# Attention on one core: one head per PSUM bank, the denominators' addition on ScalarE, and the weight conversion elsewhere in the order

## The chip, the cores and the metric

The kernel runs on one core of one Trainium2 chip. The metric is the device time of one execution in microseconds (us), median of several runs. The profile is of one execution; its times count from the first instruction. PE is TensorE's matmuls, PEld its weight loads, DVE VectorE, ACT ScalarE, POOL GpSimd, and SP SyncE, which issues most transfers.

## The reference

The program is linear attention with a feature map, followed by two feed-forward layers. Only the first part is touched by the change:

```python
def phi(x):                       # x: (4 batches, 8 heads, 576 tokens, 64 channels)
    proj = np.einsum('bhsd,df->bhsf', x, w_phi)          # 64 channels -> 128 features
    proj = proj - np.max(np.abs(proj), axis=-1, keepdims=True)
    return np.concatenate([np.exp(proj), np.exp(-proj)], axis=-1)
q_p, k_p = phi(q), phi(k)
kv  = np.einsum('bhsf,bhsd->bhfd', k_p, v)
z   = np.sum(k_p, axis=2)
num = np.einsum('bhsf,bhfd->bhsd', q_p, kv)
den = np.einsum('bhsf,bhf->bhs', q_p, z)[..., None] + 1e-06
attn = num / den
...
x = attn as (2304 tokens, 512)
g = h * clip(h + 3, 0, 6) / 6 with h = x @ w_in;  x = g @ w_out        # 512 -> 2048 -> 512
# then a mixture of 8 experts with a gate, on the same 2304 tokens
```

## The kernel before, in words

Attention works on 16 units `u`, each a pair of heads of one batch (576 tokens each). A unit's k and q come in one load as 9 blocks of 128 columns: blocks 0 to 3 are k, block 4 holds the last 64 tokens of both heads of k and of q, blocks 5 to 8 are q. The rows (partitions) of the blocks are 64 channels twice. Before the change, row half `e` of block `a` holds token block `2a + e` of the flat list of both heads' eight blocks, so each half holds blocks of both heads.

`proj` (lines 230 to 258) multiplies both row halves with `w_phi`, four 64x64 matmuls at a time, into two PSUM banks `pj`, one per row half; then, bank after bank, VectorE takes the maximum of the absolute values (line 257) and subtracts it (line 258) into `dd`, where `e` is the third index. It runs for three groups of blocks: P0 (k, four blocks), P1 (block 4), P2 (q, four blocks). `kexp` (E0, E1: one head each; E2: the rest) takes exponentials of `dd` and of its negative into `kp` on ScalarE (lines 265, 266). `kv_mm` (KV, line 280) multiplies `kp` with `v`, the two heads into two column halves, head 0 first in each round. `z_sum` (S0, S1, line 290) adds on GpSimd, and `z_mm` (Z, line 300) sums over tokens on TensorE, behind KV in the same bank `pkv`. `kv_cp` (C, line 312) copies that bank to SBUF on ScalarE, `kv_tr` (KT) transposes it, sums the z halves on VectorE (line 323) and copies the rest on ScalarE to `kvz` (line 331). `q_tr` (Q0, Q1, Q2) transposes q's part of `dd` and takes its exponentials (lines 344, 349) to `qp`. `num` (N0, N1, line 395) and `den` (D, line 359) are the two products; the addition of 1e-6 is on VectorE (line 369), and a transfer turns the result to `rt`. One period later `den2` (R) takes the reciprocal (line 376), writes it to DRAM, reads it back spread over rows as `rr` (line 381), and, in its second step, GpSimd multiplies the numerators with it (line 385).

Meanwhile the weights of the first feed-forward layer are converted from float64 bits in 16 pieces, one a period, by `split_w` (lines 132 to 169). It is a generator whose first step is the load. Its next four, each called "w" in the order, are: absolute value on ScalarE (line 154) with a maximum on GpSimd (line 155); a shift on VectorE (line 157); a second VectorE operation (line 159); a third (line 161) with two on GpSimd (lines 168, 169). The intermediates `f` and `m` have one buffer each, the raw words two.

The order on TensorE, VectorE, ScalarE and GpSimd is written out by hand as a list of names and kept; the transfers of SP are ordered by the program's scheduler. A period of iteration `it` finishes unit `it` and prepares unit `it + 1`:

```python
seq = ("KV Z C Q0 Q0 Q1 Q1 Q2 Q2 KT KT KT R P0 P0 E0 S0 E1 S1 P1 P1 E2 P2 P2 w "
       "N0 N0 N1 N1 D D w R w w").split()
```

A name that stands twice or three times is a generator: its first place issues the first part (matmuls, transposes, transfers), its later ones the evacuations. In iteration 14 the D are left out; in iteration 15 (`seq15`) they come as `d`. PSUM has eight buffers under the tag "b", given out in turn. After iteration 15 the feed-forward layer begins; its instructions are not in the hand-written order.

Of the kernel before, what the change touches and what calls it, by code (L numbers as in the profile page):

```python
# [17 lines left out]
P = 128  # L18
# [171 lines left out]
def step(g):  # L190
    return next(g, None)
# [7 lines left out]
def attention(tc, a, ident, xT, wA, rt_last, late):  # L199
    nc = tc.nc  # L200
    with ExitStack() as ctx:
# [4 lines left out]
        pl = E(name="apl", bufs=2, side="left")  # L206
        p3 = E(name="ap3", bufs=1, side="left")
        ps = E(name="aps", bufs=1, space=PS)
        wbd = cst.tile([P, 256], F32, name="wbd")
        ones = cst.tile([P, 3, 32], F32, name="ones")  # L210
        nc.gpsimd.memset(ones, 1.0)
        nc.gpsimd.memset(ones[64:128, 1, :], 0.0)
# [3 lines left out]
        def load(u):  # L216
            x = p2.tile([P, 9, P], F32, tag="qk", bufs=2, name=f"qk{u}")
            if u == 0:
                nc.sync.dma_start(wbd, a["w_phi"])
                for g in range(3):  # L220
                    nc.sync.dma_start(x[:, 3 * g : 3 * g + 3], a["qk"][u][:, 384 * g : 384 * g + 384])
            else:
                nc.sync.dma_start(x.rearrange("p n t -> p (n t)"), a["qk"][u])
            t = p2.tile([P, 10, 64], F32, tag="lv", bufs=4, name=f"v{u}")
            nc.sync.dma_start(t.rearrange("p n d -> p (n d)"), a["v"][u])
            return [x, t]
# [3 lines left out]
        def proj(u, g):  # L230
            x = lds[u][0]
            if g == 0:
                st[u] = (
                    p2.tile([P, 9, 2, P], F32, tag="dd", name=f"dd{u}"),
                    p2.tile([P, 5, 2, 2, P], F32, tag="kp", name=f"kp{u}"),
                    p2.tile([P, 18], F32, tag="mx", name=f"mx{u}"),
                )
            dd, kp, mx = st[u]
            b0, n = ((0, 4), (4, 1), (5, 4))[g]
            pj = [ps.tile([P, 512], F32, tag="b", bufs=8, name=f"pj{u}_{g}_{e}") for e in range(2)]  # L240
            for j in range(n):
                for c in range(2):
                    for e in range(2):
                        rs, cs = slice(64 * e, 64 * e + 64), slice(64 * c, 64 * c + 64)
                        nc.tensor.matmul(  # L245
                            pj[e][cs, P * j : P * j + P],
                            x[rs, b0 + j, cs],
                            wbd[rs, P * e : P * e + P],
                            start=True,
                            stop=True,  # L250
                            tile_position=(64 * e, 64 * c),
                        )
            yield
            for e in range(2):
                pv = pj[e][:, 0 : P * n].rearrange("p (x f) -> p x f", f=P)
                m = mx[:, 9 * e + b0 : 9 * e + b0 + n]
                nc.vector.tensor_reduce(m, pv, axis=AX.X, op=ALU.max, apply_absolute_value=True)  # L257
                nc.vector.tensor_sub(dd[:, b0 : b0 + n, e], pv, m.unsqueeze(2).broadcast_to([P, n, P]))  # L258

        def kexp(u, g):  # L260
            dd, kp, mx = st[u]
            if g < 2:
                dv = dd[:, 2 * g : 2 * g + 2].rearrange("p a h f -> p (a h) f")
                kv_ = kp[:, 2 * g : 2 * g + 2].rearrange("p r h s f -> p (r h) s f")
                nc.scalar.activation(kv_[:, :, 0, :], dv, AF.Exp)
                nc.scalar.activation(kv_[:, :, 1, :], dv, AF.Exp, scale=-1.0)  # L266
            elif g == 2:
                nc.scalar.activation(kp[:, 4, 0, 0, :], dd[:, 4, 1, :], AF.Exp)
                nc.scalar.activation(kp[:, 4, 0, 1, :], dd[:, 4, 1, :], AF.Exp, scale=-1.0)
# [63 lines left out]
        def q_tr(u, h):  # L333
            dd = st[u][0]
            if h == 0:
                bk.setdefault(u, {})["qp"] = p3.tile([P, 2, 2, S], F32, tag="qp", name=f"qp{u}")
            qp = bk[u]["qp"]
            pq = ps.tile([P, 512], F32, tag="b", bufs=8, name=f"pq{u}_{h}")
            if h < 2:
                for r in range(4):  # L340
                    nc.tensor.transpose(pq[:, P * r : P * r + P], dd[:, 5 + 2 * h + r // 2, r % 2, :], ident)
                yield
                for s in range(2):
                    nc.scalar.activation(qp[:, s, h, 0:512], pq, AF.Exp, scale=1.0 - 2 * s)
            else:
                nc.tensor.transpose(pq[:, 0:128], dd[:, 4, 0, :], ident)
                yield
                for s in range(2):
                    nc.scalar.activation(
                        qp[:, s, :, 512:576], pq[:, 0:128].rearrange("p (h t) -> p h t", h=2), AF.Exp, scale=1.0 - 2 * s  # L350
                    )

        def den(u):
            zs, qp = bk[u]["zs"], bk[u]["qp"]
            pd = ps.tile([P, 512], F32, tag="b", bufs=8, name=f"pd{u}")
            for s in range(2):
                for g in range(4):
                    h, c = divmod(g, 2)
                    nc.tensor.matmul(
                        pd[32 * g : 32 * g + 32, 0:288],  # L360
                        zs[:, s, h, :],
                        qp[:, s, h, 288 * c : 288 * c + 288],
                        start=(s == 0),
                        stop=(s == 1),
                        tile_position=(0, 32 * g),
                    )
            yield
            dn = pl.tile([P, 288], F32, tag="dn", name=f"dn{u}")
            nc.vector.tensor_scalar_add(dn, pd[:, 0:288], 1e-6)
            rt = pl.tile([P, 9], F32, tag="rt", name=f"rt{u}") if u < NU - 1 else rt_last  # L370
            (nc.sync if u < NU - 1 else nc.gpsimd).dma_start(rt, dn[0:128:32, :].rearrange("g (j k) -> g j k", k=9))
            rts[u] = rt
# [14 lines left out]
        def num(u, c):  # L387
# [16 lines left out]

        lds, cv = {}, {}
        seq = (
            "KV Z C Q0 Q0 Q1 Q1 Q2 Q2 KT KT KT R P0 P0 E0 S0 E1 S1 P1 P1 E2 P2 P2 w "
            "N0 N0 N1 N1 D D w R w w"
        ).split()
        pre1 = "P0 P0 E0 S0 E1 S1 P1 P1 E2 P2 P2".split()  # L410
        seq14 = [op for op in seq if op != "D"]
        seq15 = "w KV Z C Q0 Q0 d Q1 Q1 d Q2 Q2 KT KT KT R w N0 N0 N1 N1 D D w R w".split()
        with tc.manual_schedule(
            engines={nc.tensor.engine, nc.vector.engine, nc.scalar.engine, nc.gpsimd.engine}
        ):
            for it in range(-1, NU):
# [9 lines left out]
                    cv[it + 1] = split_piece(tc, p3, a, wA, 0, it + 1, ("wf", "wm", 1))  # L426
                    step(cv[it + 1])
                gens = {}
                for op in {-1: pre1, NU - 2: seq14, NU - 1: seq15}.get(it, seq):
                    kd, i = op[0], int(op[1]) if op[-1].isdigit() else 0  # L430
                    if op in gens:
                        step(gens[op])
                    elif kd == "P" and nx:
                        gens[op] = proj(it + 1, i)
                        step(gens[op])
                    elif kd == "E" and nx:
                        kexp(it + 1, i)
                    elif kd == "R" and it >= 1:
                        gens[op] = den2(it - 1)
                        step(gens[op])  # L440
                    elif kd == "S" and nx:
                        z_sum(it + 1, i)
                    elif kd == "Z" and has:
                        z_mm(it)
                    elif kd == "C" and has:
                        kv_cp(it)
                    elif op == "w" and has:
                        step(cv[it])
                    elif op == "KV" and has:
                        kv_mm(it)  # L450
                    elif kd == "d":
                        gens[op] = den(it - 1)
                        step(gens[op])
                    elif has and kd in "KQND":
                        gens[op] = {"K": kv_tr, "D": den}[kd](it) if kd in "KD" else {"Q": q_tr, "N": num}[kd](it, i)
                        step(gens[op])
# [727 lines left out]
def lay_out(arrays):  # L1184
# [4 lines left out]
    q, k, v = pair(q), pair(k), pair(v)  # L1189
    qk = np.empty((NU, 2, D, 9, P), np.float32)  # L1190
    for n, x in ((0, k), (5, q)):
        x = x[:, :, 0:512].reshape(NU, 4, 2, P, D)
        qk[:, :, :, n : n + 4] = x.transpose(0, 2, 4, 1, 3)
    for i, x in enumerate((q, k)):
        qk[:, i, :, 4] = x[:, :, 512:].transpose(0, 3, 1, 2).reshape(NU, D, P)
    vv = np.zeros((NU, P, 10, D), np.float32)
    vv[:, :, 0:8] = v[:, :, 0:512].reshape(NU, 2, 4, P, D).transpose(0, 3, 1, 2, 4).reshape(NU, P, 8, D)
    wb = np.zeros((P, 2, P), np.float32)
    for h in range(2):
        vv[:, 64 * h : 64 * h + 64, 8 + h] = v[:, h, 512:]  # L1200
        wb[64 * h : 64 * h + 64, h] = w
    return {"in_qk": qk.reshape(NU, P, 9 * P), "in_v": vv.reshape(NU, P, 10 * D), "in_w_phi": wb.reshape(P, 2 * P)}


_INS = [
# [23 lines left out]
```

## Time and profile before

| what | value |
|---|---|
| median of 3 runs | 927.88 us (927.8 to 929.29) |
| the profiled execution: its own time, its span | 926.54 us, 924.5 us |
| PE, DVE, ACT, POOL busy | 882.1, 589.2, 496.4, 349.0 us |
| mean granted TensorE clock | 0.992 of full speed |
| attention | to about 196 us |

A busy share is an average over stages with different limits; the ends of matmuls are modelled, so short waits of TensorE show better in the starts of its instructions and in PEld's idle time than in PE's busy time.

### The profile page before, as it was taken

The page shows a single profiled execution, that of the slowest core. Times are in us where ns is not written, and L with a number is a line of the kernel's source. Part 1 is how long each engine was busy: PE and PEld are TensorE (multiplying, and loading weights), DVE is VectorE, ACT ScalarE, POOL GpSimd, SP SyncE. Part 2 cuts the span into 40 slices and gives each one's busy share as a digit, 9 for nine tenths or more (in the row PEclk, how much of TensorE's full clock was granted, in tenths as well). Part 3 has the DMA queues.
Part 4 walks back from the last instruction along what each step waited for, and adds up shares of the span by engine and source line. Part 5 has one row for each costly group of instructions (what it writes and reads, how often), then busy time and mean ns, then how long its engine had stood idle before and what let it go on. Part 6 is the DMA issues. An engine that isn't in the chain of part 4 may idle for free. (4 is left out here: it accounts for less than half of the span.)

```text
span 924.5 us, 16115 instructions
## 1 busy us (share of the span) xinstructions
PE 882.1 (95%) x5890; PEld 712.8 (77%) x5890; DVE 589.2 (64%) x998; ACT 496.4 (54%) x869; POOL 349.0 (38%) x244
## 2 busy tenths in 40 slices
PE   7999999979989999999999999999699999999996
PEld 4666666557878998898898988987578888888884
DVE  5888888879993433433433333456598888888882
ACT  4666666644443233233233233244488888888882
POOL 2566666654660100100000000113457766666631
PEclk9999999999999999999999999999799999999999
DMA  7454554333410200100100100541324651545530
GB/s 238 117 167 146 153 162 133 100 105 121 121 47 1 67 3 0 35 1 1 35 1 1 35 1 1 98 141 19 61 93 162 244 197 37 215 144 194 192 133 15
DMA packets 39247, 86.37 MB, mean 93 GB/s; under 512 B 10868, under 2 KB 11896, under 8 KB 39164
## 3 DMA queue, kind: packets, MB, share of 16 engines
q1 hardware_dynamic: 34332, 75.81, 26.4%
q0 software_dynamic: 4832, 9.48, 3.1%
q8 instruction: 48, 0.79, 0.4%
q14 instruction: 35, 0.29, 0.1%
HBM read 130.38 MB, written 11.44 MB: 153 GB/s over the span
## 5 line engine op out<-in xcount | busy, mean ns | idle before, releaser
L503 DVE SCALAR_TENSOR_TENSOR t<-t,ph 128x384 f32<-128x384 f32 x96 | 53.1, 553 | 160.5 <-ACT t L502 160.5
L502 ACT ACTIVATE t<-ph,b 128x384 f32<-128x384 f32 x96 | 55.6, 579 | 166.4 <-PE ph L500 166.4
L640 POOL DMA_INDIRECT lst<-ids,pi x18 | 17.9, 995 | 237.5 <-DVE pi L637 231.1
L508 ACT ACTIVATE gh<-t 128x384 fp32r<-128x384 f32 x96 | 50.4, 525 | 83.5 <-DVE t L503 80.6
L807 DVE TENSOR_TENSOR wl<-raw,wh 128x1024 fp32r<-128x1024 f32 x63 | 76.2, 1246 | 5.7 <-ACT wh L806 5.5
L512 DVE TENSOR_TENSOR gl<-t,gh 128x384 fp32r<-128x384 f32 x86 | 48.4, 563 | 46.1 <-ACT gh L508 45.0
L806 ACT ACTIVATE wh<-raw 128x1024 fp32r<-128x1024 f32 x72 | 73.0, 1069 | 1.0 <-DMA raw<-in_moe_w 1.0
L500 PE MATMUL ph<-xh,wi0A 128*128 128x384 f32 x192 | 67.5, 352 | 4.9 <-DVE t L503 3.2
L500 PE MATMUL ph<-xl,wi0A 128*128 128x384 f32 x192 | 64.7, 337 | 1.2 <-DVE xl L491 1.2
L500 PE MATMUL ph<-xh,wi1B 128*128 128x384 f32 x192 | 64.7, 337 | 0.9 <-POOL wi1B L169 0.9
L500 PE MATMUL ph<-xh,wi0B 128*128 128x384 f32 x192 | 64.9, 338 | 0.0
L500 PE MATMUL ph<-xh,wi1A 128*128 128x384 f32 x192 | 64.6, 337 | 0.0
L500 PE MATMUL ph<-xl,wi0B 128*128 128x384 f32 x192 | 64.5, 336 | 0.0
L290 POOL TENSOR_TENSOR ks<-kp 128x512 f32<-128x512 f32 x32 | 41.1, 1307 | 50.4 <-ACT kp L266 50.4
L527 PE MATMUL po<-wo1B,gh 128*128 128x512 f32 x144 | 57.3, 398 | 1.3 <-POOL wo1B L169 1.3
L527 PE MATMUL po<-wo0B,gh 128*128 128x512 f32 x144 | 57.1, 396 | 0.6 <-ACT wo0B L166 0.6
L280 PE MATMUL pkv<-kp,v 128*64 128x256 f32 x320 | 48.3, 387 | 9.0 <-ACT kp L266 8.5
L527 PE MATMUL po<-wo1A,gh 128*128 128x512 f32 x144 | 56.7, 394 | 0.0
L527 PE MATMUL po<-wo0A,gh 128*128 128x512 f32 x144 | 56.7, 393 | 0.0
L257 DVE TENSOR_REDUCE mx<-pj 128x4 f32<-128x512 f32 (+1 forms) x96 | 52.0, 541 | 7.3 <-PE pj L245 7.3
L258 DVE TENSOR_TENSOR dd<-pj,mx 128x512 f32<-128x512 f32 (+1 forms) x96 | 53.6, 558 | 4.3
L807 DVE TENSOR_TENSOR wi1A<-raw,wi0A 128x1024 fp32r<-128x1024 f32 x42 | 50.1, 1221 | 5.4 <-ACT wi0A L806 5.0
(242 smaller groups left out, 2322.2 us busy)
## 6 DMA issues: line engine op xcount, KB each, us to landing
raw<-in_moe_w SPq DMA_DIRECT2D x168, 512.0 KB
qk<-in_qk SPq DMA_DIRECT2D x15, 576.0 KB
raw_i<-in_moe_w_in SPq DMA_DIRECT2D x16, 512.0 KB
raw_o<-in_moe_w_out SPq DMA_DIRECT2D x16, 512.0 KB
v<-in_v SPq DMA_DIRECT2D x16, 320.0 KB
x2d<-rows SPq DMA_DIRECT2D x18, 256.5 KB
rr<-rscr SPq DMA_DIRECT2D x30, 144.0 KB
x2d<-zr SPq DMA_DIRECT2D x3, 256.5 KB
```

What stands on the lines that cost most here:

```text
L257: nc.vector.tensor_reduce(m, pv, axis=AX.X, op=ALU.max, apply_absolute_value=True)
L258: nc.vector.tensor_sub(dd[:, b0 : b0 + n, e], pv, m.unsqueeze(2).broadcast_to([P, n, P]))
L280: nc.tensor.matmul(pkv[64 * h : 64 * h + 64, 0:256], l, m.rearrange("p s f -> p (s f)"), start=(r == 0), stop=(r == 4))
L290: nc.gpsimd.tensor_add(ks, k[:, :, 0], k[:, :, 1])
L500: nc.tensor.matmul(ph[:, 0:T], l[:, d, fs], r[:, d, :], start=(d == 0 and i == 0), stop=(d == 3 and i == 2))
L502: nc.scalar.activation(g, ph[:, 0:T], AF.Relu, bias=b3)
L503: nc.vector.scalar_tensor_tensor(g, g, 6.0, ph[:, 0:T], op0=ALU.min, op1=ALU.mult)
L508: nc.scalar.activation(gh, g, AF.Copy)
L512: (nc.gpsimd if 4 < n < 15 else nc.vector).tensor_sub(gl, g, gh.bitcast(F32))
L527: nc.tensor.matmul(pos[c][j], l[:, js], wo[r], start=(f == 0 and r == 0 and l is gh), stop=(f == 15 and l is gl))
L806: nc.scalar.activation(hi, raw[i], AF.Copy)
L807: (nc.gpsimd if i == 7 or (s, i) == (0, 6) else nc.vector).tensor_sub(lo, raw[i], hi.bitcast(F32))
```

## The change

The inputs are laid out so that row half `e` is head `e`: each bank of `pj` then holds one head, and E0, E1, Q0 and Q1 read one value of `dd`'s third index. The projection weights are the same matrix twice, without the second column block. Unit 0's load is cut into pieces of 2, 2 and 5 blocks instead of 3, 3 and 3. The addition of 1e-6 is a ScalarE activation with a bias tile `eps`. In the order, Q2's exponentials stand behind the copy to `kvz`; R's second step, the multiplication on GpSimd, stands ahead of P2 instead of near the end; the three later steps of the conversion stand together behind P2, and its absolute value and maximum are done at the end of the period before ("a"; in iteration 0, which has no period before with one, behind C, as "b").

```diff
-        wbd = cst.tile([P, 256], F32, name="wbd")
+        wbd = cst.tile([P, P], F32, name="wbd")
+        eps = cst.tile([P, 1], F32, name="eps")
+        nc.vector.memset(eps, 1e-6)
...
-                for g in range(3):
-                    nc.sync.dma_start(x[:, 3 * g : 3 * g + 3], a["qk"][u][:, 384 * g : 384 * g + 384])
+                for b0, b1 in ((0, 2), (2, 4), (4, 9)):
+                    nc.sync.dma_start(x[:, b0:b1], a["qk"][u][:, P * b0 : P * b1])
...
-                            wbd[rs, P * e : P * e + P],
+                            wbd[rs, :],
...
-                dv = dd[:, 2 * g : 2 * g + 2].rearrange("p a h f -> p (a h) f")
-                kv_ = kp[:, 2 * g : 2 * g + 2].rearrange("p r h s f -> p (r h) s f")
+                dv = dd[:, 0:4, g]
+                kv_ = kp[:, 2 * g : 2 * g + 2].rearrange("p a e s f -> p (a e) s f")
...
-                    nc.tensor.transpose(pq[:, P * r : P * r + P], dd[:, 5 + 2 * h + r // 2, r % 2, :], ident)
+                    nc.tensor.transpose(pq[:, P * r : P * r + P], dd[:, 5 + r, h, :], ident)
...
-            nc.vector.tensor_scalar_add(dn, pd[:, 0:288], 1e-6)
+            nc.scalar.activation(dn, pd[:, 0:288], AF.Identity, bias=eps)
...
-            "KV Z C Q0 Q0 Q1 Q1 Q2 Q2 KT KT KT R P0 P0 E0 S0 E1 S1 P1 P1 E2 P2 P2 w "
-            "N0 N0 N1 N1 D D w R w w"
+            "KV Z C Q0 Q0 Q1 Q1 Q2 KT KT KT Q2 R P0 P0 E0 S0 E1 S1 P1 P1 E2 R P2 P2 w w w "
+            "N0 N0 N1 N1 D D a"
...
+        seq0 = "KV Z C b".split() + seq[3:]
...
-        seq15 = "w KV Z C Q0 Q0 d Q1 Q1 d Q2 Q2 KT KT KT R w N0 N0 N1 N1 D D w R w".split()
+        seq15 = "KV Z C Q0 Q0 d Q1 Q1 d Q2 KT KT KT Q2 R w w w N0 N0 N1 N1 D D R".split()
...
-                for op in {-1: pre1, NU - 2: seq14, NU - 1: seq15}.get(it, seq):
+                for op in {-1: pre1, 0: seq0, NU - 2: seq14, NU - 1: seq15}.get(it, seq):
...
-                    elif op == "w" and has:
+                    elif op in ("w", "b"):
                         step(cv[it])
+                    elif op == "a":
+                        step(cv[it + 1])
...
-        x = x[:, :, 0:512].reshape(NU, 4, 2, P, D)
-        qk[:, :, :, n : n + 4] = x.transpose(0, 2, 4, 1, 3)
+        qk[:, :, :, n : n + 4] = x[:, :, 0:512].reshape(NU, 2, 4, P, D).transpose(0, 1, 4, 2, 3)
```

## Rows read from the trace of the kernel before

**Rows 1.** Busy us (x instructions) of PE, PEld, DVE, ACT, POOL by stretch; clock, DMA.

```profile
16.00:176.00 160.00, 154.81 (x2085) 96.99 (x2085) 135.64 (x254) 98.96 (x238) 100.35 (x81) 1.00 0.47 142
```

**Rows 2.** Order of time, PE, 11 to 177 us: start, us, what, count, idle before.

```profile
11.16 2.37 PE L280 MATMUL pkv<-kp,v 128*64 128x256 f32 x18 [0.39 <-ACT kp L266]
16.03 2.34 PE L245 MATMUL pj<-wbd,qk 64*64 64x128 f32 x72
...
27.07 2.40 PE L245 MATMUL pj<-wbd,qk 64*64 64x128 f32 x72
...
107.39 2.40 PE L245 MATMUL pj<-wbd,qk 64*64 64x128 f32 x72
109.72 2.16 PE L395 MATMUL po<-qp,kvz 128*64 128x288 f32 x16
111.81 1.18 PE L359 MATMUL pd<-qp,zs 128*32 128x288 f32 x16
112.92 0.65 PE L280 MATMUL pkv<-kp,v 128*64 128x256 f32 x2
113.93 2.37 PE L280 MATMUL pkv<-kp,v 128*64 128x256 f32 x18 [0.37 <-ACT kp L266]
116.23 0.40 PE L300 MATMUL pkv<-ks,ones 128*32 128x256 f32 x1
...
118.80 2.40 PE L245 MATMUL pj<-wbd,qk 64*64 64x128 f32 x72
...
176.36 2.40 PE L245 MATMUL pj<-wbd,qk 64*64 64x128 f32 x72
```

**Rows 3.** Waits, 16 to 176 us: who waited for whom, us, times, longest.

```profile
PEld pkv L280 <- ACT kp L266: 18.7, 28, 0.8
```

**Rows 4.** Order of time, VectorE, ScalarE and GpSimd in the period around 112 us.

```profile
108.79 0.20 DVE L376 RECIPROCAL rt<-rt 128x9 f32<-128x9 f32 x1
...
108.91 0.62 DVE L257 TENSOR_REDUCE mx<-pj 128x4 f32<-128x512 f32 x1
...
109.64 0.69 DVE L258 TENSOR_TENSOR dd<-pj,mx 128x512 f32<-128x512 f32 x1
...
110.97 0.69 DVE L258 TENSOR_TENSOR dd<-pj,mx 128x512 f32<-128x512 f32 x1
...
111.69 0.63 ACT L265 ACTIVATE kp<-dd 128x512 f32<-128x512 f32 x1 [2.40 <-DVE dd L258]
...
113.27 0.61 ACT L266 ACTIVATE kp<-dd 128x512 f32<-128x512 f32 x1
...
114.66 0.69 DVE L258 TENSOR_TENSOR dd<-pj,mx 128x512 f32<-128x512 f32 x1
...
116.98 0.43 DVE L157 TENSOR_SCALAR f_i<-m_i 128x512 uint32<-128x512 uint32 x1 [1.26 <-POOL m_i L155]
...
117.40 0.60 ACT L312 ACTIVATE kvs<-pkv 128x512 f32<-128x512 f32 x1 [1.95 <-PE pkv L300]
117.43 1.42 POOL L385 TENSOR_TENSOR xT<-xT,rr 128x576 f32<-128x576 f32 x1 [0.49 <-DMA rr<-rscr]
117.44 1.96 DVE L159 SCALAR_TENSOR_TENSOR f_i<-raw_i,f_i 128x512 uint32<-128x512 uint32 x1
...
119.43 0.69 DVE L161 SCALAR_TENSOR_TENSOR f_i<-raw_i,f_i 128x512 uint32<-128x512 uint32 x1
```

**Rows 5.** Order of time in the attention's last period and the first feed-forward matmul.

```profile
187.72 0.70 ACT L154 ACTIVATE m_o<-raw_o 128x512 f32<-128x512 f32 x1 [3.19 <-DVE f_o L157]
...
191.52 2.16 PE L395 MATMUL po<-qp,kvz 128*64 128x288 f32 x16 [1.91 <-ACT kvz L331]
...
196.53 0.41 PE L500 MATMUL ph<-xh,wi0A 128*128 128x384 f32 x1 [1.74 <-DVE dn L369]
```

**Rows 6.** Groups by line, 0 to 300 us: count, busy us, mean ns, idle before.

```profile
L403 ACT ACTIVATE xT<-po 128x288 f32<-128x288 f32 x32 | 11.1, 393 | 0.2
...
L369 DVE TENSOR_SCALAR dn<-pd 128x288 f32<-128x288 f32 x16 | 7.2, 448 | 0.0
```

More of the change, by code (lines that the diff above doesn't have):

```diff
@@ L1197, in lay_out @@
     vv[:, :, 0:8] = v[:, :, 0:512].reshape(NU, 2, 4, P, D).transpose(0, 3, 1, 2, 4).reshape(NU, P, 8, D)
-    wb = np.zeros((P, 2, P), np.float32)
     for h in range(2):
         vv[:, 64 * h : 64 * h + 64, 8 + h] = v[:, h, 512:]
-        wb[64 * h : 64 * h + 64, h] = w
-    return {"in_qk": qk.reshape(NU, P, 9 * P), "in_v": vv.reshape(NU, P, 10 * D), "in_w_phi": wb.reshape(P, 2 * P)}
+    return {"in_qk": qk.reshape(NU, P, 9 * P), "in_v": vv.reshape(NU, P, 10 * D), "in_w_phi": np.concatenate([w, w])}
 _INS = [
```

## The prediction

> **What bounds the kernel now.** I read the table of stretches first, then the waits of the attention loop, then the order of time. The loop from 16 to 176 us has TensorE busy 154.8 of 160 us, ScalarE 99.0, VectorE 135.6, GpSimd 100.4 [rows 1]; the reader is to see that TensorE looks full while nobody else is. The rest of the span, from 196.53 us on, is feed-forward and expert work that the diff does not touch.
>
> The loop has 14 periods from the projection that starts at 16.03 to the one at 176.36, that is 160.33 us or 11.45 us each [rows 2]. Busy shares hide where that comes from, so I took one period apart, the one from 107.39 to 118.80 (11.41 us) [rows 2]: projections to denominators 4.42 us, denominators to the first kv matmul 1.11, first kv matmul to the other kv matmuls 1.01, those to the key sums 2.30, key sums to the next projection 2.57. The third piece is a wait: two kv instructions go, and then the weight load waits for the second pair of exponentials of k (E1; 0.37 us of it shows as an idle matrix row, because the ends of matmuls are modelled). The waits row says the same for the loop: 18.7 us of weight-load idle in 28 waits, two a period [rows 3].
>
> How long would the kv matmuls take without it? The two heads go to different column halves, so they run in pairs. Sixteen numerator instructions of the same kind, four pairs of two-pass matmuls on 288 columns, take 2.09 us (109.72 to 111.81), 0.52 a pair; on 256 columns that is 0.465, and five pairs are 2.32. The eighteen instructions behind the wait take 2.30 [rows 2]: they are five rounds already, the lone second half of round one being a round by itself. So the whole 1.01 would go. If it were not so (nine half rounds at 0.256), 0.76 would go. The floor of a period is 4.42 + 1.11 + 2.31 + 2.57 = 10.41 us, at worst 10.67.
>
> Why E1 is late is to be read from the other engines in the same period [rows 4]. P0's reduction starts at 108.91, 1.52 us after the projection; its two banks are 1.33 us apart (subtractions at 109.64 and 110.97); E0 starts at 111.69, with the subtraction of the second bank, after ScalarE idled 2.40 us; E1's last exponential starts at 113.27 and takes 0.61; the kv matmuls go at 113.93. Two delays are in this. E0 waits for both banks, as each holds blocks of both heads. And VectorE is late for P0: it finishes the previous weight piece between, one step of which took 1.96 us beside GpSimd's multiplication at 117.43. In the first period, 16.03 to 27.07, 11.04 us, VectorE was not late [rows 2]: so its order costs about 0.41 of the 1.04 us between 11.45 and 10.41, the layout of the banks the rest.
>
> **The change part by part.**
>
> *One head per bank.* Same matmuls, same sizes; E0 reads bank 0 alone and goes 1.33 us earlier, E1 follows bank 1. Order after it, counted from the start of a projection: P0 at 1.15 (0.37 earlier, where VectorE is free; an estimate: 16 of the 36 equal steps of the 2.33 us from 107.39 to 109.72 are 1.04, and 0.1 for the last to come out), E0 at 1.15 + 1.42 = 2.6, done 3.75; second bank at 3.9, E1 done 5.1. The first kv matmul is due at 4.42 + 1.11 = 5.53. So both are there, with 0.4 us to spare, and TensorE has no wait left.
>
> *Weight conversion after P2, its first step a period ahead.* VectorE's three steps (w w w) no longer wait for GpSimd's maximum; that was done at the end of the period before. P2's last subtraction starts at 114.66 [rows 4], 5.75 after P0's first reduction, so it ends at about 1.15 + 6.4 = 7.6 in the new count; the steps of 0.43, 0.69 and 0.69 end at 9.4; the next VectorE work is due at 10.5, when the kv transposes are done. That hides them, with 1.1 us of cover. New wait: the ScalarE absolute value ("a", 0.70 us [rows 5]) writes the one buffer m, which the first w still reads until 8.0; so it ends at 8.7, and queued behind it stands the copy C, due when the key sums are done, at 117.40 − 116.23 = 1.17 after 7.84, that is 9.0. Cover 0.3 us. If it goes, C, the exponentials of q and the numerators are late by what is over.
>
> *R's multiplication on GpSimd, moved ahead of the conversion's two GpSimd steps.* It waits for rr, which came 8.64 us after the reciprocal (108.79 to 117.43) [rows 4], through three transfers on SP's queue. The reciprocal is next due at 0.5 to 0.7, so rr at about 9.2. Behind it on GpSimd stand the two conversion steps, the maximum and the next S0 and S1, all of which with it are GpSimd's whole period, 100.4/14 = 7.2 us [rows 1]: S1 would end at 16.4, and the key sums are due at 10.41 + 7.84 = 18.25. Cover 1.8 us. SP's issues per period stay the same; the weight load now follows a conversion that ends at 9.4, ahead of the reciprocal's transfer, and holds up nothing.
>
> *Moved together, GpSimd and VectorE meet less.* The 1.96 us step ran beside GpSimd's multiplication, 0.69 without [rows 4]. In the new order the multiplication comes at 9.2, when the steps are nearly over, so I take the short durations. The Trainium skill, "SBUF — State Buffer", section "Who interferes with whom", has it that VectorE operations with two SBUF inputs, or in a two-port mode, and GpSimd operations exclude each other for a whole instruction, and that operations with one SBUF input don't. The trace agrees: the step at 117.44, begun 0.01 us after the multiplication's 1.42 [rows 4], lost 1.27. By the rule a conversion step that starts just behind the multiplication would lose all of it, which is the second rival below.
>
> *Denominators' addition on ScalarE.* Off VectorE 0.448 us, on ScalarE about the 0.393 of a copy of the same shape [rows 6]; between 0.39 and the 0.70 of the absolute value on 512 columns. ScalarE idles 1.95 us before C [rows 4], so no cost. The Trainium skill, "ScalarE: Activation LUTs", section "Rules for kernel authors", says the opposite: additions belong on VectorE. An estimate from that page's formula with a pointer bias is 0.52 us; the sum would be the same, as either fits in the 1.95 us.
>
> *Q2's exponentials after kvz.* Both end where they ended, in swapped order; the numerators need both. No cost: ScalarE was done with both 1.90 after the projection (111.69 − 2.40 − 107.39), and E0 is due at 2.6.
>
> *Start.* The first kv matmuls waited for E1 too (11.16) [rows 2]: 1.33 off for the bank, and smaller first pieces and half the projection weights may bring a little; 0 to 0.6, I take 0.2. But in iteration 0 the absolute value stands right behind C, ahead of the exponentials: up to 0.70 back; I take 0.55.
>
> *End.* From 176.36 to the first feed-forward matmul at 196.53 are 20.17 us. Numerators waited 1.91 for kvz there, the first feed-forward matmul 1.74 for the denominators' addition on VectorE, and ScalarE 3.19 for a conversion step in front of C [rows 5]. The kv wait gives 1.0 as in the loop; of the 1.91 I take 1.2, since the addition for unit 14 now sits on ScalarE ahead of kvz; of the 1.74 I take 0.7, as VectorE's w steps are now queued behind a reciprocal that waits for its transfer, and ahead of xl. Together 2.9, between 0.5 and 4.6.
>
> *Sum.* Loop: with a period of 10.45, near the floor, 146.3 instead of 160.3, −14.0 (−10.9 at 10.67, −14.6 at 10.41). Start −1.5, iteration 0 +0.55, end −2.9: −17.85. The profiled execution took 926.54 us for its span of 924.5, so 908.7; it was 1.34 below the median of the runs, so I say 910. Its own range with these bounds is 905 to 915.
>
> **The rivals.** First: the program's dependency tracking takes the interleaved halves of dd as one, so E0 still waits for both banks. Then only the order helps, and the period becomes that of the first one, 11.04: −5.7 in the loop, start and iteration 0 +0.3, end −2: about 920.5. For it speaks only that no instruction in the trace reads one half while the other is being written; against it, that each write and read names its own half.
>
> Second: the absolute value blocks ScalarE. If the first w falls beside a GpSimd instruction and takes about 1.3 us longer, as the 1.96 against 0.69 shows, it eats the 0.3 of cover and the period is 10.45 + 1.0 = 11.45, no gain in the loop; with start and end the result is about 924. The row of 117.44 shows that the price is real; the distance worked out to the multiplication (1.2 us) speaks against it.
>
> Third, slower: rr comes late on GpSimd. It decides from 1.8 us past 9.2, and each us beyond is paid once a period; past 2.8 the loop is slower than now. If SP's in-order queue put the rr transfer behind the weight load that waits for the last w (9.4), rr would land half of the 8.64 after that (an estimate: two transfers, one after the other), at 13.7, the key sums 2.7 late, the period 13.15: +23.8 in the loop, about 948. Against it: in the trace of now the multiplication waits for rr only 0.49 us [rows 4], though the last w ends at 119.43 + 0.69, ahead of the next reciprocal; both stand in the same order after the change.
>
> **How the numbers follow.** Forecast 0.70; first rival 0.11; second 0.07 (split between faster and same); third 0.08 (a slow case, with near misses that end level); the rest, about 0.04, levels out for reasons I don't see. Faster 0.87, same 0.05, slower 0.08; 0.2%, 1.9 us, is about what a measurement of this kernel can tell from no change. The range runs from 905 to 921, which takes in the first rival: below it nearly nothing, above it the late rivals.
>
> **What would show it.** Right: the kv wait for E1 gone from TensorE's rows, E0 starting with the second bank's reduction, projections 10.4 to 10.7 us apart, conversion steps never above 0.75 us, the first feed-forward matmul near 178.5. Wrong: E0 still behind the second subtraction; the absolute value ending after the key sums; GpSimd's multiplication past 11 us into the period with the key sums waiting for ks.

## The result, and the profile after

The changed kernel took 911.85 us (median; 911.27 to 912.51), the kernel before 928.38 on the same chip: ratio 0.9821, 95% interval 0.9807 to 0.9836. A second comparison on another chip gave 0.9833 (0.9818 to 0.9848). The span of the profiled execution fell from 924.5 to 909.9 us, by 14.6. Lines after the change are two to five higher: the projection is L247, the subtraction L260, the kv matmul L282.

First TensorE's order of time, the start of the loop and one of its periods (start, us, what, count, idle before); it answers to [rows 2].

```profile
14.71 1.52 PE L247 MATMUL pj<-wbd,qk 64*64 64x128 f32 x42
...
25.52 2.40 PE L247 MATMUL pj<-wbd,qk 64*64 64x128 f32 x72
...
36.52 2.45 PE L247 MATMUL pj<-wbd,qk 64*64 64x128 f32 x72
...
98.98 2.40 PE L247 MATMUL pj<-wbd,qk 64*64 64x128 f32 x72
...
103.40 1.18 PE L361 MATMUL pd<-qp,zs 128*32 128x288 f32 x16
104.50 2.38 PE L282 MATMUL pkv<-kp,v 128*64 128x256 f32 x20
106.81 0.40 PE L302 MATMUL pkv<-ks,ones 128*32 128x256 f32 x1
...
109.38 2.40 PE L247 MATMUL pj<-wbd,qk 64*64 64x128 f32 x72
...
161.38 2.40 PE L247 MATMUL pj<-wbd,qk 64*64 64x128 f32 x72
```

All twenty kv instructions now go at once, 1.10 us after the denominators, and take 2.31 to the key sums. The period is 4.42 + 1.10 + 2.31 + 2.57 = 10.40 us. Two periods are clearly longer: 10.81 (from 14.71) and 11.00 (from 25.52). The view of waits, 14 to 160 us, answers to [rows 3]: of 18.7 us in 28 waits this is left, and it shows on the weight loads alone; no matmul waits for E1.

```profile
PEld pkv L282 <- ACT kp L268: 5.6, 12, 0.5
```

The other engines in that period, in order of time, against [rows 4].

```profile
99.43 0.21 DVE L378 RECIPROCAL rt<-rt 128x9 f32<-128x9 f32 x1
...
100.13 0.69 DVE L259 TENSOR_REDUCE mx<-pj 128x4 f32<-128x512 f32 x1 [0.50 <-PE pj L247]
...
101.65 0.63 ACT L267 ACTIVATE kp<-dd 128x512 f32<-128x512 f32 x1 [0.81 <-DVE dd L260]
...
102.25 0.69 DVE L260 TENSOR_TENSOR dd<-pj,mx 128x512 f32<-128x512 f32 x1
...
103.51 0.61 ACT L268 ACTIVATE kp<-dd 128x512 f32<-128x512 f32 x1
...
105.95 0.69 DVE L260 TENSOR_TENSOR dd<-pj,mx 128x512 f32<-128x512 f32 x1
106.56 0.42 DVE L157 TENSOR_SCALAR f_i<-m_i 128x512 uint32<-128x512 uint32 x1
...
107.01 0.69 DVE L159 SCALAR_TENSOR_TENSOR f_i<-raw_i,f_i 128x512 uint32<-128x512 uint32 x1
107.01 0.72 ACT L154 ACTIVATE m_i<-raw_i 128x512 f32<-128x512 f32 x1 [1.48 <-DVE f_i L157]
...
107.88 1.82 POOL L387 TENSOR_TENSOR xT<-xT,rr 128x576 f32<-128x576 f32 x1 [2.37 <-DMA rr<-rscr]
107.98 0.60 ACT L314 ACTIVATE kvs<-pkv 128x512 f32<-128x512 f32 x1 [0.25 <-PE pkv L302]
```

The reduction of P0 starts 1.15 us after the projection and now waits for TensorE, not the other way round; E0 starts before the second bank's subtraction, and E1 is done (104.12) before the kv matmuls are due. The absolute value waits for the first conversion step and ends 0.25 us ahead of the copy C.

Then the end of attention, TensorE's order of time, against [rows 5], and the stretches there (length; busy us of PE, PEld, DVE, ACT, POOL; granted clock; DMA).

```profile
174.55 2.16 PE L397 MATMUL po<-qp,kvz 128*64 128x288 f32 x16 [1.77 <-ACT kvz L333]
...
179.04 0.44 PE L505 MATMUL ph<-xh,wi0A 128*128 128x384 f32 x1 [1.22 <-ACT xh L495]
...
180.73 0.44 PE L505 MATMUL ph<-xl,wi0A 128*128 128x384 f32 x1 [1.07 <-DVE xl L496]
...
181.93 0.52 PE L505 MATMUL ph<-xl,wi0A 128*128 128x384 f32 x1
```

```profile
179.00:181.60 2.60, 1.49 (x7) 1.17 (x8) 2.58 (x4) 1.23 (x3) 2.17 (x2) 1.00 0.75 219
181.60:185.10 3.50, 3.50 (x13) 3.50 (x12) 2.45 (x6) 1.17 (x2) 0.67 (x1) 0.53 0.82 225
...
189.00:199.00 10.00, 9.41 (x47) 7.91 (x46) 9.15 (x14) 4.41 (x9) 4.00 (x3) 1.00 0.41 122
199.00:209.00 10.00, 9.32 (x46) 7.73 (x45) 9.10 (x13) 4.17 (x8) 3.94 (x3) 1.00 0.34 105
```

The feed-forward layer starts 17.49 us earlier than before (179.04 against 196.53). But its first matmuls wait, a stretch of 3.5 us runs at the lower clock, and then VectorE is busy 9.1 to 9.2 of 10 us. ScalarE's first activation of each feed-forward block shows what is left (before, then after; first and ninth block).

```profile
198.93 0.58 ACT L502 ACTIVATE t<-ph,b 128x384 f32<-128x384 f32 x1 [3.77 <-PE ph L500]
...
236.60 0.57 ACT L502 ACTIVATE t<-ph,b 128x384 f32<-128x384 f32 x1
```

```profile
183.54 0.57 ACT L507 ACTIVATE t<-ph,b 128x384 f32<-128x384 f32 x1
...
221.57 0.56 ACT L507 ACTIVATE t<-ph,b 128x384 f32<-128x384 f32 x1
```

The ninth block is 15.03 us earlier, not 17.49. From the last projection it is 236.60 − 176.36 = 60.24 us before and 221.57 − 161.38 = 60.19 after: in this kernel the end of attention gave nothing that lasted.

### The profile page after: what moved, and what is told of

Same layout as the page of the kernel before. It is cut to its first block, busy times and chain, and to the rows that moved or that the text cites. A ratio compares the mean times of both kernels' runs of the same rounds, so it can differ in the third digit from the quotient of the medians.

```text
span 909.9 us, 16128 instructions
## 1 busy us (share of the span) xinstructions
PE 874.5 (96%) x5890; PEld 711.5 (78%) x5890; DVE 578.3 (64%) x983; ACT 505.0 (56%) x885; POOL 351.2 (39%) x244
## 5 line engine op out<-in xcount | busy, mean ns | idle before, releaser
L645 POOL DMA_INDIRECT lst<-ids,pi x18 | 17.7, 984 | 237.2 <-DVE pi L642 230.8
L260 DVE TENSOR_TENSOR dd<-pj,mx 128x512 f32<-128x512 f32 (+1 forms) x96 | 53.6, 558 | 4.3
L812 DVE TENSOR_TENSOR wo1A<-raw,wo0A 128x1024 fp32r<-128x1024 f32 x41 | 50.9, 1276 | 3.3 <-ACT wo0A L811 3.2
L816 POOL DMA_INDIRECT pre<-lst,gi x22 | 38.3, 1740 | 30.0 <-DMA lst<-ids,pi 15.2
```

Source lines behind the costliest of these rows:

```text
L645: sc = nc.gpsimd.indirect_dma_start(lst, bass.IndirectOffsetOnAxis(ap=pi[:, j : j + 1], axis=0), ids[:, m : m + 1], None, bounds_check=NL - 1,
L812: (nc.gpsimd if i == 7 or (s, i) == (0, 6) else nc.vector).tensor_sub(lo, raw[i], hi.bitcast(F32))
L816: nc.gpsimd.indirect_dma_start(pre[:, s : s + 1], None, lst, bass.IndirectOffsetOnAxis(ap=gi[:, s : s + 1], axis=0), bounds_check=NL - 1, ...
```

## The experiments

My theory after the result: E0 and E1 waiting for both banks is what cost the loop its microsecond; the order and ScalarE's addition are worth less than their share of the diff; what the end of attention won is lost to VectorE behind it. The rivals are written at each run. Times are medians, ratios are to the kernel before on the same chip.

**The order without the layout.** The changed kernel with the old layout of blocks.

```diff
-                dv = dd[:, 0:4, g]
+                dv = dd[:, 2 * g : 2 * g + 2].rearrange("p a h f -> p (a h) f")
...
-                    nc.tensor.transpose(pq[:, P * r : P * r + P], dd[:, 5 + r, h, :], ident)
+                    nc.tensor.transpose(pq[:, P * r : P * r + P], dd[:, 5 + 2 * h + r // 2, r % 2, :], ident)
...
-        qk[:, :, :, n : n + 4] = x[:, :, 0:512].reshape(NU, 2, 4, P, D).transpose(0, 1, 4, 2, 3)
+        x = x[:, :, 0:512].reshape(NU, 4, 2, P, D)
+        qk[:, :, :, n : n + 4] = x.transpose(0, 2, 4, 1, 3)
```

> The changed kernel with the old layout of the banks: blocks of both heads in each bank, E0 waits for both subtractions; the new order, ScalarE's addition and the smaller first pieces stay. My theory (the layout carries about 0.63 us a period, the order 0.41): projections 11.0 to 11.1 us apart instead of 10.40, the wait for E1 back at about 0.6 us, the run about 9 to 10 us above the changed kernel, some 921. Rival (the wait came from VectorE being late, and the order alone cures it): 10.4 us apart, 912.

924.86 us, ratio 0.9964 (0.9949 to 0.9978). The loop runs from 16.95 to 172.42: 14 periods of 11.10 us, as expected, with the kv matmuls late again. The run is 4 us above what I said: the loop starts 0.92 us later than in the kernel before, and no gain of the end is left. TensorE's order of time in one period:

```profile
83.55 2.40 PE L247 MATMUL pj<-wbd,qk 64*64 64x128 f32 x72
...
89.07 3.09 PE L282 MATMUL pkv<-kp,v 128*64 128x256 f32 x20
...
94.65 2.40 PE L247 MATMUL pj<-wbd,qk 64*64 64x128 f32 x72
```

**The layout without the order.** The kernel before with the three edits above the other way round, nothing else.

> The kernel before with one head per bank, and nothing else of the change. If the two parts add up as the prediction's first part has it (0.41 for the order, 0.63 for the layout): projections 10.8 us apart, about 918. If they are two cures for one wait: E0 and E1 1.33 us earlier is more than the 1.0 us that TensorE waited, the wait is gone with VectorE's order unchanged, projections 10.4 to 10.5 apart, and the run is at 912 to 914, so that the new order is worth little on top.

909.69 us, ratio 0.9802 (0.9780 to 0.9824). Its loop, from the first of these two rows to the second, is 146.63 us long; that of the changed kernel 146.67.

```profile
15.12 2.34 PE L245 MATMUL pj<-wbd,qk 64*64 64x128 f32 x72
...
161.75 2.40 PE L245 MATMUL pj<-wbd,qk 64*64 64x128 f32 x72
```

So these are two cures for one wait, and the layout alone is the whole of the loop's gain. Some of its periods are longer (10.86 from 77.75), where the reciprocal waits for rt, as in this row of VectorE's order of time:

```profile
79.62 0.21 DVE L376 RECIPROCAL rt<-rt 128x9 f32<-128x9 f32 x1 [1.34 <-DMA rt<-dn]
```

Beside the changed kernel on one chip, in five rounds:

> The changed kernel itself on the chip of this call, for the comparison with the next run: 0.982 of the kernel before.

> One head per bank alone, again, in more rounds, beside the changed kernel on the same chip. If the order and ScalarE's addition add nothing (loops of 146.6 and 146.7 us in the two profiles): the same as the changed kernel within 0.2%, or up to 2 us faster, as its first time was. If they are worth something: slower by more than 2 us.

The changed kernel 912.19 us, 0.9833 (0.9818 to 0.9848); the layout alone 909.96 us, 0.9807 (0.9794 to 0.9821). The three edits of layout beat the whole change by 2.2 us; the intervals overlap by a little (0.9818 to 0.9821), so its sign is likely and its size is not settled. Against the kernel before both are plain.

The two profiles show where such a difference comes from. In the layout alone, in order of time, SP issues the first loads of the next weights, ScalarE makes xh (the first input of the feed-forward layer), VectorE takes the first step on the loaded weights, and the ninth feed-forward block starts:

```profile
172.87 0.82 SPq L136 DMA_DIRECT2D raw_i<-in_moe_w_in  x2
...
173.60 1.40 ACT L490 ACTIVATE xh<-xT 128x384 fp32r<-128x384 f32 x3
...
177.44 0.42 DVE L142 TENSOR_SCALAR f_i<-raw_i 128x512 uint32<-128x512 uint32 x1
...
218.89 0.57 ACT L502 ACTIVATE t<-ph,b 128x384 f32<-128x384 f32 x1
```

In the changed kernel the last unit's addition waits on ScalarE for the denominators. The load is issued only behind it (the view of waits puts 1.6 us of the load's wait down to it), and xh stands behind it in ScalarE's order:

```profile
177.92 0.50 ACT L371 ACTIVATE dn<-pd,eps 128x288 f32<-128x288 f32 x1 [0.71 <-PE pd L361]
...
178.50 0.34 SPq L136 DMA_DIRECT2D raw_i<-in_moe_w_in  x1
178.51 1.76 ACT L495 ACTIVATE xh<-xT 128x384 fp32r<-128x384 f32 x4
...
182.77 0.43 DVE L142 TENSOR_SCALAR f_i<-raw_i 128x512 uint32<-128x512 uint32 x1 [0.65 <-DMA raw_i<-in_moe_w_in]
...
221.38 0.57 ACT L507 ACTIVATE t<-ph,b 128x384 f32<-128x384 f32 x1
```

Counted from the last projection (160.70 and 161.42), VectorE's first step comes 16.74 us after it in the layout alone and 21.35 in the changed kernel, the ninth block 58.19 and 59.96. The profiles of the other runs below, all but the one without the mask, which has less work there, side with these two. From its first feed-forward matmul to its ninth block a kernel takes 39.6 to 40.3 us in all five profiles with the last addition on VectorE, the kernel before (40.07) among them, and 42.3 to 43.3 in all eight with it on ScalarE. From the last projection the ninth block of the kernel before is at 60.24, that of the layout alone at 58.73 and 58.19 (its two profiles). So the layout alone keeps 1.5 to 2.1 us of the end, and the changed kernel loses them to its own addition. Whether the late load or the late xh costs more was not separated.

**The addition back on VectorE.**

```diff
-            nc.scalar.activation(dn, pd[:, 0:288], AF.Identity, bias=eps)
+            nc.vector.tensor_scalar_add(dn, pd[:, 0:288], 1e-6)
```

> The changed kernel with the denominators' addition back on VectorE. The prediction's step (0.45 us moved between two engines that both have room): no change in the loop, 912 within 1. Rival: in the new order the addition stands behind the three conversion steps on VectorE, so it ends at about 9.9 us into the period, its transfer lands near 12, the reciprocal waits for it in front of P0's reduction, and the wait for E1 comes back: projections 10.6 to 11.1 apart, 3 to 9 us above the changed kernel.

947.59 us, ratio 1.0197 (1.0178 to 1.0216): 35 us above the changed kernel, and far more than either theory said. The mechanism is the rival's. In order of time on VectorE and SP's queue:

```profile
88.65 1.79 DVE L161 SCALAR_TENSOR_TENSOR f_o<-raw_o,f_o 128x512 uint32<-128x512 uint32 x1
...
90.37 0.45 DVE L371 TENSOR_SCALAR dn<-pd 128x288 f32<-128x288 f32 x1
...
90.93 0.60 SPq L373 DMA_DIRECT2D rt<-dn  x1
...
94.16 0.22 DVE L378 RECIPROCAL rt<-rt 128x9 f32<-128x9 f32 x1 [3.01 <-DMA rt<-dn]
```

The addition stands behind the third conversion step, the reciprocal waits 3.01 us for rt, and behind the reciprocal stands P0: its reduction starts at 94.29, 4.32 us after the projection at 89.97 instead of 1.15. That makes the next conversion steps late too. After the first (10.80) the periods are 12.2 to 14.2 us.

**The same, but ahead of the conversion steps.** Beside the edit above, the end of the order:

```diff
-            "... E1 S1 P1 P1 E2 R P2 P2 w w w "
-            "N0 N0 N1 N1 D D a"
+            "... E1 S1 P1 P1 E2 R P2 P2 "
+            "N0 N0 N1 N1 D D w w w a"
```

> The changed kernel with the denominators' addition on VectorE as in the run that was 35 us slower, but ahead of the three conversion steps in its order. If that run was slow since the addition stood behind the steps, so that its transfer kept the reciprocal, and P0 behind it, waiting 3 us: projections 10.4 to 10.6 us apart again, the run within 3 us of the changed kernel. Rival (VectorE has no room for the 0.45 us): 12 us or more apart again.

910.10 us, ratio 0.9807 (0.9792 to 0.9822); all periods are 10.39 to 10.43 but two, 10.81 (from 14.70) and 10.67 (from 108.74). So it was the place in VectorE's queue, not the 0.45 us. The ninth feed-forward block (217.98) stands 56.97 us behind the last projection (161.01). ScalarE was needed for the order that was written, not for room.

**ScalarE's addition in the old order.** One head per bank, halved projection weights, the addition on ScalarE; against the layout alone:

```diff
-        wbd = cst.tile([P, 256], F32, name="wbd")
+        wbd = cst.tile([P, P], F32, name="wbd")
...
-                            wbd[rs, P * e : P * e + P],
+                            wbd[rs, :],
...
-            nc.vector.tensor_scalar_add(dn, pd[:, 0:288], 1e-6)
+            nc.scalar.activation(dn, pd[:, 0:288], AF.Identity, bias=eps)
```

> One head per bank, the halved projection weights and the denominators' addition on ScalarE for all units; the order of before. Theory (the addition costs nothing on either engine as long as it stands ahead of the conversion steps): projections 10.40 us apart as with the layout alone; the end of attention is shorter by about 1.5 us, since the first feed-forward matmul no longer waits 2.03 us for the addition on VectorE: 908 to 909. Rival (the addition on ScalarE is what the changed kernel loses at the end, ahead of kvz): 0.5 to 1 us slower than the layout alone.

911.87 us, ratio 0.9831 (0.9804 to 0.9859). The periods are 10.35 to 10.40 and the first feed-forward matmul is at 178.60, 1.57 us earlier than in the first profile of the layout alone. Of that 1.10 was there at the last projection; from the last projection (160.65) it is 17.95 us instead of 18.42, so the end is 0.47 shorter and not 1.5. Yet the run is not faster: the ninth block (221.93) stands 61.28 us behind the last projection, 3.1 more than in the second profile of the layout alone. That is the rival's direction, but not its place: what the addition holds up is xh and the next weights' load (issued at 178.07), as above, not kvz.

**Smaller first pieces, and ScalarE's addition for the last unit alone,** on the layout with the halved weights.

```diff
-                for g in range(3):
+                for b0, b1 in ((0, 2), (2, 4), (4, 9)):
...
-            nc.vector.tensor_scalar_add(dn, pd[:, 0:288], 1e-6)
+            if u < NU - 1:
+                nc.vector.tensor_scalar_add(dn, pd[:, 0:288], 1e-6)
+            else:
+                nc.scalar.activation(dn, pd[:, 0:288], AF.Identity, bias=eps)
```

> One head per bank, the smaller first pieces and halved projection weights, the order of before, and the addition on ScalarE for the last unit alone. Theory: start 0.4 us earlier than the layout alone (the changed kernel's first E0 was at 7.32), end 1.5 us earlier, and if the half clock behind the attention (3.7 us, about 1.7 us of time) comes from TensorE idling there, part of that too: 906 to 908, below both kernels. Rival (the half clock stays, or moves): 908.

912.18 us, ratio 0.9832 (0.9804 to 0.9859). That is above what theory and rival said. No half clock, first feed-forward matmul at 178.17, and its ninth block at 220.95, 60.35 us after the last projection at 160.60. The stretch at the lower clock is therefore not what costs there. Behind the last projection this kernel differs from the layout alone (58.19 and 58.73) only in the last unit's addition, so that addition on ScalarE costs some 2 us by the ninth block: the load is issued at 177.64, VectorE's first step on it is at 182.34.

**The last conversion earlier,** in iteration 15.

```diff
-        seq15 = "... KT KT KT Q2 R w w w N0 N0 N1 N1 D D R".split()
+        seq15 = "... KT KT KT Q2 w w w R N0 N0 N1 N1 D D R".split()
```

> The changed kernel with the last piece's three conversion steps ahead of the last R in iteration 15, while VectorE waits 3.0 us for the transfer to rt. Theory: the first feed-forward matmuls then get xl about 1 us earlier, since GpSimd's subtraction of the last piece no longer runs beside the first xl, and with TensorE idling less the stretch at half clock behind them (3.5 us, 1.6 us of time) is gone or shorter: 1 to 2.7 us below the changed kernel. Rival: the half clock comes from something else and stays: at most 1 us, or nothing.

913.91 us, ratio 0.9850 (0.9832 to 0.9868): not faster, against the theory; by these intervals (0.9807 to 0.9836 for the changed kernel) it is not clearly slower either. The wait for xl is gone, but VectorE's first step on the next weights is at 183.41, no earlier than before (182.95), its product for the first block stands behind these steps, and a matmul at 186.61 waits 2.58 us for it instead. A wait moved.

**Iteration 0's absolute value later** (behind E2 instead of behind C).

```diff
-        seq0 = "KV Z C b".split() + seq[3:]
+        seq0 = [x for op in seq for x in ((op, "b") if op == "E2" else (op,))]
```

> The changed kernel with iteration 0's absolute value behind E2 instead of behind C. Theory: the 0.41 us that the first period (14.71 to 25.52, 10.81 us) is longer than the others goes, and nothing else moves: first period 10.4, the run 0.4 us below the changed kernel, which is near what the measurement can tell, so the period decides. Rival (the first period is long since the loads are late): 10.8 as before.

912.70 us, ratio 0.9833 (0.9811 to 0.9856). The first period is 10.34 instead of 10.81, as expected; but the last projection is at 161.34 instead of 161.38, since a later period took 11.1. What happened there is the prediction's second rival, once, in the order of time of the engines:

```profile
63.80 1.41 POOL L387 TENSOR_TENSOR xT<-xT,rr 128x576 f32<-128x576 f32 x1 [1.00 <-DMA rr<-rscr]
63.84 1.66 DVE L157 TENSOR_SCALAR f_o<-m_o 128x512 uint32<-128x512 uint32 x1
...
65.53 0.70 ACT L154 ACTIVATE m_o<-raw_o 128x512 f32<-128x512 f32 x1 [2.73 <-DVE f_o L157]
66.13 0.59 ACT L314 ACTIVATE kvs<-pkv 128x512 f32<-128x512 f32 x1
...
66.77 0.66 PE L321 MATMUL pk<-ident,kvs 128*128 128x128 f32 x4 [0.48 <-ACT kvs L314]
```

GpSimd's multiplication starts 0.04 us ahead of the first step, which takes 1.66 instead of 0.42; the absolute value waits for it, C for that, and TensorE for C.

**TensorE kept busy in the end** (iteration 15: Q2's first step between the KT, its transpose 16 times).

```diff
-                nc.tensor.transpose(pq[:, 0:128], dd[:, 4, 0, :], ident)
+                for _ in range(16 if u == NU - 1 else 1):
+                    nc.tensor.transpose(pq[:, 0:128], dd[:, 4, 0, :], ident)
...
-        seq15 = "KV Z C Q0 Q0 d Q1 Q1 d Q2 KT KT KT Q2 R w ...".split()
+        seq15 = "KV Z C Q0 Q0 d Q1 Q1 d KT Q2 KT KT Q2 R w ...".split()
```

> The changed kernel, and in iteration 15 alone Q2's transposes behind KT's and done 16 times over (the same values), which fills most of TensorE's 1.77 us wait for kvz. If the half clock at 181.6 to 185.1 follows from TensorE idling in the attention's end: it is gone or shorter, the run up to 1.6 us below the changed kernel. If it comes from something else: it stays, and the run is level or a little slower.

911.79 us, ratio 0.9819 (0.9794 to 0.9843). TensorE's wait for kvz is gone (busy 4.00 of 4 us from 170 to 174), and the half clock comes all the same, from 180.73 on. So here it does not follow from idling before 174 us; the last section says how little one profile tells of it.

**Less VectorE work in the feed-forward's start.** The last step of the 16 conversions there, which sets tiny weights to zero, is left out.

```diff
-        nc.vector.scalar_tensor_tensor(
-            m, m, TINYB * TINYB, f.bitcast(F32), op0=ALU.is_ge, op1=ALU.mult
-        )
-        f = m
+        f = f.bitcast(F32)
```

> The changed kernel without the last VectorE step (the mask that sets tiny values to zero) of each of the 16 conversions of the second half of the first layer's weights, which run while the feed-forward layer starts: weights below the threshold come out wrong. Theory (the time won at the end of attention is given back, since VectorE, 9.1 to 9.7 of 10 us busy there, sets the pace of the first sixteen feed-forward blocks): ninth block 3 us or more earlier than the 60.19 us it stands behind the last projection now, the run 3 to 8 us below the changed kernel. Rival (TensorE or the loads set the pace): ninth block at 60.2, the run level.

901.64 us, ratio 0.9702 (0.9685 to 0.9719), 10 us below the changed kernel. The third to seventh blocks start 4.0 us apart (193.07 to 209.09) instead of 4.8 (193.41 to 212.61), the ninth at 216.88, 55.70 after the last projection at 161.18. VectorE sets the pace there in the changed kernel. The pace shows it, not the busy share: with less work a block VectorE is still busy 9.2 of 10 us, and now TensorE is full (stretch, then PE, PEld, DVE, ACT, POOL; clock; DMA).

```profile
199.00:209.00 10.00, 10.00 (x52) 8.97 (x51) 9.23 (x15) 5.62 (x11) 3.82 (x3) 1.00 0.41 121
```

The edit also takes a link out of the chain from the load to the weights. The two were not separated, but the waits of TensorE in the changed kernel's third and fourth block (0.25 and 0.34 us, at 191.92 and 196.71) are for VectorE's product, not for weights.

## Why the prediction was right, and where it was not

It said 910 and faster; the median is 911.85. Step by step:

- *The wait for E1 and its size.* Right. Five rounds of kv matmuls, 2.31 us, and a floor of 10.41 were read from the rows; the period is 10.40. The loop gave 160.33 − 146.67 = 13.66 us; with iteration 0 the prediction had 13.45.
- *"Its order costs about 0.41 of the 1.04 us a period, the layout of the banks the rest".* Wrong as a division. The order alone gives 11.45 − 11.10 = 0.35, the layout alone 0.98 of 0.98. E0 1.33 us earlier is more than TensorE waited, so VectorE may be late and nothing is lost.
- *The addition, "so no cost".* Right in the loop: 0.502 us on ScalarE, hidden. I had taken 0.39, from a copy without a bias; the estimate by the Trainium skill's "ScalarE: Activation LUTs", section "What ACT_TABLE_LOAD costs", was 0.52, and the measurement is nearer to that. But the step looked only at the engines' time, and not at what stands behind the addition if it stays: 35 us hang on its place in VectorE's queue, and in the last period, on ScalarE, the next weights' load and xh stand behind it: some 2 us by the ninth feed-forward block.
- *Start and iteration 0.* −1.32 us to the first loop projection (I had −1.5), and the first period 0.41 too long (I had 0.55). Taking the 0.41 away did not shorten the loop.
- *End, "together 2.9".* The waits were read rightly up to the first feed-forward matmul: 20.17 became 17.66, −2.51. But the sum went on as if all later work moved with it. By the ninth block −0.05 is left. This is the term that failed, and with it the addition's "no cost". Behind the attention VectorE is the bound, as the run without the mask shows, and its first step on the next weights comes 21.57 us after the last projection, 18.50 in the kernel before: TensorE starts earlier and waits for it. The end was not worthless: with the addition on VectorE that step comes after 16.7 to 17.7 us, and 1.5 to 3.3 us last to the ninth block.
- *"So I take the short durations".* Not so, and nearly without cost. Of the 42 conversion steps in the loop's 14 periods seven took 1.56 to 1.91 us instead of 0.42 to 0.69, each begun while GpSimd's multiplication ran, which came earlier than the 9.2 us worked out (7.4 to 8.4 into these periods). "Never above 0.75 us" was not met; six of the seven were hidden.
- *Second rival, the absolute value blocking ScalarE.* It is real, and struck once, as the first of the three steps has to be the one that meets the multiplication: in the changed kernel it accounts for the 11.00 us period, where the first step at 33.10 took 1.56 us beside the multiplication at 32.97. One period of 14 paid 0.6 us, not all. The Trainium skill's "SBUF — State Buffer", section "Who interferes with whom", has whichever starts first keep the shared port; the trace agrees, 1564 ns in that one, 416 in the median of its group.
- *Third rival, rr late on GpSimd.* Its multiplication waited 22.2 us for rr in twelve periods, and TensorE never for ks: the cover held. The row of the view of waits, of the changed kernel from 14 to 160 us (sum, count, longest):

```profile
POOL xT L387 <- DMA rr<-rscr: 22.2, 12, 3.8
```

In spans: 1.32 + 13.66 + 0.05 = 15.03 us at the ninth block, and 14.6 at the end; the 0.4 between stays open. The sum had 17.85; nearly all of the 2.8 that it was too high is the end.

## What to carry to other kernels

Two edits that shorten the same wait don't add up: run each alone before keeping both. An addition of 0.45 us can be worth 35 us by what is queued behind it, when a transfer and a reciprocal hang on it. And before a gain at the end of a stage is counted, ask which engine sets the pace of the next one, and whether its work starts earlier too: here VectorE's did not, since an addition of 0.5 us on another engine stood ahead of what it waits for.

## What was not expected of the hardware

In the changed kernel TensorE's granted clock was 0.53 from 181.6 to 185.1 us, mostly at the lower of its two levels: ten matmuls took 0.52 us instead of 0.34. The edit alone does not decide this. In the second profile of the same kernel the same stretch ran at 1.00:

```profile
181.60:185.10 3.50, 3.31 (x19) 2.99 (x17) 2.67 (x6) 1.16 (x2) 0.71 (x1) 1.00 0.79 230
```

Of the two profiles of the layout alone one has such a stretch and the other has not. So nothing here shows what brings it or removes it, and the run with the filled wait does not either. It cost little: the ninth block stands 60.19 us behind the last projection with it and 59.96 without, 58.73 and 58.19 in the layout alone.
